# The last four rows of a weight quarter, loaded by partitions: 112 at once, then four times four

## The chip, the cores and the metric

The kernel runs on one core of one Trainium2 chip. The metric is the device time of one execution in microseconds (us).

## The reference

It is one step of grouped-query attention with a cache: 32 query heads, 8 key and value heads, a cache of 2048 positions, 8 batches with 4 tokens each, in bf16.

```python
B, Sq, D = 8, 4, 512            # x
Hq, Hkv, Sk, Dh = 32, 8, 2048, 128
q = (x @ wq).reshape(B, Sq, Hq, Dh).transpose(0, 2, 1, 3)
k = repeat(k_cache, Hq // Hkv, axis=1)
v = repeat(v_cache, Hq // Hkv, axis=1)
scores = einsum("bhqd,bhkd->bhqk", q, k) * Dh ** -0.5
p = softmax(scores)
o = einsum("bhqk,bhkd->bhqd", p, v)
out = o.transpose(0, 2, 1, 3).reshape(B, Sq, Hq * Dh) @ wo
```

## The kernel before, in words

The work is cut into 16 units, each one batch with four of the eight key/value heads (`units`). For each unit the kernel loads a K tile and a V tile of 2 MiB each (`load_k`, `load_v`), 128 partitions by 16 KB. VectorE turns the keys (`turn_keys`), TensorE makes the scores, ScalarE the exponentials, and the probabilities go back into the order of the keys (`probs_to_keys`) as copies that write 32 partitions each of one buffer. TensorE multiplies them with V (`values`); `divide` and `finish` scale and transpose the result. The loop over `n` runs 18 times: at step n it makes the scores of unit n and the values of unit n - 2.

All loads are issued by SyncE (SP), in the order of the program. `load_ready` issues the K and V tiles as their buffers come free (three of each). The last V tile is loaded in two parts, three quarters and one quarter. At step 15, behind all K and V loads, come the loads of wo, by the list `pieces`.

wo has 4096 rows of 512 elements (1024 bytes). It is taken in four quarters of 1024 rows; within a quarter, partition q holds the eight rows 8q to 8q + 7, which lie side by side in memory. `load_wo(p, r0, n)` loads the rows r0 to r0 + n - 1 of each partition's eight in quarter p:

```python
pieces = [(0, 0, 8), (1, 0, 8), (2, 0, 8), (3, 0, 4), (3, 4, 2), (3, 6, 2)]
```

The first three are 1 MiB each. The fourth, (3, 0, 4), is half of the last quarter: 128 partitions with 4096 adjoining bytes each, 512 KB. The last two are 256 KB each.

After the loop `project(p, r0, n)` multiplies the attention result with the rows of one piece, two matmuls for each r, and adds everything up in one accumulator, `out_ps`. The pieces come in the order of the list, and steps of the last unit's finishing (`finish`, `to_tokens`, `to_wo_rows`) stand between the first ones. One copy takes `out_ps` to `out_sb`, and two stores of 16 KB, one from ScalarE's queue and one from SP's, end the program. The order on each engine is the one written out (`manual_schedule`); waits between engines are put in where one instruction needs the data or the buffer of another.

Of the kernel before, what the change touches and what calls it, by code (L numbers as in the profile page):

```python
# [14 lines left out]
def kernel(  # L15
# [9 lines left out]
    nc = tc.nc  # L25
# [16 lines left out]
    NP = Hq // HP  # L42
    DH = D // 2
    NU = (Hkv // G) * B
    KB, VB, PB, LAG = 3, 3, 2, 2
    scale = float(Dh) ** -0.5
    AX = mybir.AxisListType.X
    ADD = mybir.AluOpType.add
# [52 lines left out]
    def load_wo(p, r0, n):  # L101
        rows = wo[p * HP * 128 : (p + 1) * HP * 128, :].rearrange("(q r) j -> q r j", r=WR)
        w0 = p * WR + r0
        nc.sync.dma_start(wo_sb[:, w0 : w0 + n, :], rows[:, r0 : r0 + n, :])

    load_k(0)
    nc.sync.dma_start(wq_sb[:, :, :], wq.rearrange("(p r) n -> p r n", r=R))
# [94 lines left out]
    wo_sb = wpool.tile([128, NP * WR, D], BF16, tag="w", name="wo_sb")  # L202
# [174 lines left out]
    for n in range(NU + LAG):  # L377
# [37 lines left out]
        if n == NU - 1:  # L415
            assert not loads, loads
            for piece in pieces:
                load_wo(*piece)
# [46 lines left out]
```

## Time and profile before

| what | value |
|---|---|
| median of three runs | 190.73 us (185.65 to 190.85) |
| the profiled execution | 185.65 us, span 183.9 us |
| TensorE (PE) busy | 124.5 us, 68% of the span |
| VectorE (DVE) busy | 119.3 us, 65% |
| ScalarE (ACT) busy | 83.3 us, 45% |
| GpSimd (POOL) busy | 57.2 us, 31% |
| read from memory | 75.53 MB, 411 GB/s over the span |
| share of DMA in the chain that ended last | 51% |
| mean granted TensorE clock | 0.907 |

Busy time is what an engine spent on instructions, and may lie beside that of another. The chain that ended last is followed back from the last instruction, at each step to what released it. The span is the time from the first instruction to the last; the execution's own time has 1.75 us more. DMA work is done by 16 DMA engines; a transfer has landed when the last of the engines that carry it is done.

### The profile page before, as it was taken

To read this page: it belongs to the slowest core of one execution; us is meant where nothing else is said; L and a number is where in the kernel's file an instruction comes from. 1 tells how busy PE (TensorE), PEld (TensorE's weight loads), DVE (VectorE), ACT (ScalarE), POOL (GpSimd) and SP (SyncE) were. 2 spreads that over 40 slices of the span, in tenths; PEclk is the share of its full clock that TensorE was granted. 3 is DMA by queue.
4 is the path that set the end of the run, shared out by engine and by line. 5 is a ranking of instruction groups with operands and counts; after the bars stand their busy time and mean duration, and the time that the engine had idled before them with its cause. 6 is when DMAs were issued, how large, how long until landed. Compare 5 with 4: busy or idle time off the path is not lost.

```text
span 183.9 us, 2569 instructions
## 1 busy us (share of the span) xinstructions
PE 124.5 (68%) x964; PEld 82.1 (45%) x964; DVE 119.3 (65%) x147; ACT 83.3 (45%) x154; POOL 57.2 (31%) x122
## 2 busy tenths in 40 slices
PE   0000465437959796887978858399867977499992
PEld 0000141202626574755736626247453746269770
DVE  0180234968597989989889777567857685936210
ACT  2000130272825674946847646346572638084020
POOL 8920000152405151632534515142332415056000
PEclk9999999655887999999999999958996699879999
DMA  6999999999999999999999999999999999999980
GB/s 185 471 435 389 442 417 446 417 442 428 424 442 417 446 413 437 421 435 431 428 431 428 438 413 438 438 428 435 417 442 417 442 421 435 438 411 429 421 366 19
DMA packets 5915, 75.71 MB, mean 412 GB/s; under 512 B 688, under 2 KB 784, under 8 KB 1296
## 3 DMA queue, kind: packets, MB, share of 16 engines
q1 hardware_dynamic: 5856, 75.55, 96.8%
q8 instruction: 7, 0.11, 0.2%
q14 instruction: 4, 0.03, 0.0%
q10 hardware_dynamic: 48, 0.02, 0.0%
HBM read 75.53 MB, written 0.03 MB: 411 GB/s over the span
## 4 chain that ended last, share of the span: by engine, by line
DMA 51%; DVE 30%; PE 14%; ACT 2%; issue 1%; SPq 0%; ACTq 0%; DVEq 0%
DMA k_sb<-in_k_cache_dram 24%; DVE kt L137 21%; DMA v_sb<-in_v_cache_dram 9%; DMA x_sb<-in_x_dram 9%; PE s_ps L215 9%; DMA wo_sb<-in_wo_dram 8%; DVE top L233 5%; PE o_ps L300 3%; DVE swapped L225 1%; DVE q_g L174 1%; PE psq L157 1%; DVE q_bd L193 1%; ACT q_g L172 1%; PE pse L181 1%; DVE less L239 1%
## 5 line engine op out<-in xcount | busy, mean ns | idle before, releaser
L137 DVE STREAM_TRANSPOSE kt<-k_sb 128x2048 f32<-128x2048 f32 x32 | 72.0, 2288 | 17.5 <-DMA k_sb<-in_k_cache_dram 17.4
L215 PE MATMUL s_ps<-kt,q_bd 128*64 128x512 bf16 x256 | 44.5, 479 | 33.1 <-DVE kt L137 33.1
L300 PE MATMUL o_ps<-v_sb,probs 128*128 128x256 bf16 x512 | 61.3, 281 | 0.0
L271 POOL COPY probs<-p_t 32x512 bf16<-32x512 bf16 x63 | 38.6, 612 | 59.4 <-DVE r_sb L289 57.1
L300 PEld LDWEIGHTS <-probs 128*128 128x128 bf16 x512 | 50.5, 101 | 12.1 <-issue 5.2
L271 ACT COPY probs<-p_t 32x512 bf16<-32x512 bf16 x62 | 38.1, 615 | 19.7 <-DVE r_sb L289 18.5
L215 PEld LDWEIGHTS <-q_bd 128*64 128x64 bf16 x256 | 17.3, 126 | 49.7 <-issue 25.2
L233 DVE TENSOR_REDUCE top<-s_ps 128x1 f32<-128x1024 f32 x16 | 19.6, 1224 | 16.7 <-PE s_ps L215 16.7
L251 ACT ACTIVATE s_sb<-s_ps,less 128x1024 bf16<-128x1024 f32 x16 | 22.4, 1400 | 9.8 <-DVE less L239 9.6
L225 POOL COPY l_swapped<-l_sb 64x1 f32<-64x1 f32 x32 | 5.8, 180 | 50.3 <-ACT s_sb L251 49.6
L324 ACT CAST oT<-o_t 128x64 bf16<-128x64 f32 x16 | 3.4, 212 | 33.3 <-PE o_t L323 33.3
L147 PE MATMUL xtp<-ident,x_sb 32*128 32x32 bf16 x4 | 0.3, 194 | 18.7 <-DMA x_sb<-in_x_dram 18.7
L316 ACT ACTIVATE o_sc<-o_ps,r_sb 64x128 f32<-64x128 f32 x28 | 10.1, 362 | 5.9 <-PE o_ps L300 5.7
L172 ACT ACTIVATE q_g<-psq 32x512 bf16<-32x512 f32 x4 | 2.4, 588 | 21.6 <-DVE q_g L174 21.6
L261 DVE STREAM_TRANSPOSE p_t<-s_sb 128x512 f32<-128x512 f32 x16 | 10.7, 672 | 1.6 <-ACT s_sb L251 1.6
L147 PEld LDWEIGHTS <-x_sb 32*128 32x128 bf16 x4 | 0.2, 114 | 18.7 <-DMA x_sb<-in_x_dram 18.7
L323 PEld LDWEIGHTS o_t<-both,o_sc 128*128 128x128 f32 x32 | 5.4, 211 | 7.1 <-issue 6.1
L323 PE MATMUL o_t<-both,o_sc 128*128 128x64 f32 x32 | 7.5, 320 | 0.2 <-DVE o_sc L318 0.2
L130 POOL MEMSET probs<- 128x4096 bf16 x2 | 7.0, 3511 | 0.0
L174 DVE TENSOR_SCALAR q_g<-psq 32x512 bf16<-32x512 f32 x4 | 2.7, 681 | 4.4 <-ACT q_g L172 2.3
L181 PE MATMUL pse<-ident,q_g 128*128 128x128 bf16 x32 | 3.3, 263 | 3.3 <-ACT q_g L172 2.9
L225 DVE COPY swapped<-top 64x1 f32<-64x1 f32 x32 | 4.7, 148 | 0.8
(32 smaller groups left out, 48.5 us busy)
## 6 DMA issues: line engine op xcount, KB each, us to landing
k_sb<-in_k_cache_dram SPq DMA_DIRECT2D x16, 2048.0 KB, 20.3
v_sb<-in_v_cache_dram SPq DMA_DIRECT2D x15, 2048.0 KB, 19.8
wq_sb<-in_wq_dram SPq DMA_DIRECT2D x1, 4096.0 KB, 17.3
wo_sb<-in_wo_dram SPq DMA_DIRECT2D x3, 1024.0 KB, 18.6
v_sb<-in_v_cache_dram SPq DMA_DIRECT2D x1, 1536.0 KB, 13.8
v_sb<-in_v_cache_dram SPq DMA_DIRECT2D x1, 512.0 KB, 14.6
wo_sb<-in_wo_dram SPq DMA_DIRECT2D x1, 512.0 KB, 21.3
wo_sb<-in_wo_dram SPq DMA_DIRECT2D x2, 256.0 KB, 16.9
```

The source lines that it names most:

```text
L130: nc.gpsimd.memset(pr[:, :, :, :, :, :], 0.0)
L137: nc.vector.transpose(kts[(u, t)][:, :, :, :, :].rearrange("k c h s e -> k (c h s e)").bitcast(FP32), ks[u][:, t * CT : (t + 1) * CT, :].r ...
L181: nc.tensor.matmul(pse[:, h, :, :, :].rearrange("d g b s -> d (g b s)"), lhsT=q_g[:, h, k, e, :, :].rearrange("t g w -> t (g w)"), rhs=ide ...
L215: nc.tensor.matmul(s_pss[u][h * NQ : (h + 1) * NQ, t, :, :], lhsT=q_bd[:, hq, k, e, b, :, :].rearrange("k g q -> k (g q)"), rhs=kts[(u, t) ...
L225: engine.tensor_copy(out=out[h * NQ : (h + 1) * NQ, :], in_=in_[(1 - h) * NQ : (2 - h) * NQ, :])
L233: nc.vector.reduce_max(out=top[:, :], in_=s_pss[u][:, :, :, :].rearrange("q t c s -> q (t c s)"), axis=AX,)
L251: nc.scalar.activation(out=s_sbs[u][:, :, :, :].rearrange("q a s j -> q a j s"), in_=s_pss[u][:, :, :, :].rearrange("q t (a j) s -> q (t a ...
L261: nc.vector.transpose(p_t[:, :, :, :, :].rearrange("s x g q j -> s (x g q j)").bitcast(FP32), s_sbs[u][:, :, :, :].rearrange("q a s j -> q ...
L271: by[h * G + g](out=probs[u % PB][g * S : (g + 1) * S, h, :, :, g, :], in_=p_t[quad * S : (quad + 1) * S, :, g % 2, :, :].rearrange("s x q ...
L300: nc.tensor.matmul(o_pss[u][:, :, :].rearrange("n j d -> n (j d)"), lhsT=probs[u % PB][:, h, t * CT // 4 + a, :, :, :].rearrange("s j g q ...
L316: nc.scalar.mul(out=to, in_=of, mul=by)
L323: nc.tensor.matmul(o_t[:, :], lhsT=o_scs[u][:, :], rhs=both[:, :], start=True, stop=True)
```

## The change

The load of piece (3, 0, 4) is issued as five transfers instead of one: partitions 0 to 111 in the first, then 112 to 115, 116 to 119, 120 to 123 and 124 to 127. All other pieces are loaded as before, and the same bytes go to the same places.

```diff
     KB, VB, PB, LAG = 3, 3, 2, 2
+    XE, FEW = 4, (NP - 1, 0)
...
     def load_wo(p, r0, n):
         rows = wo[p * HP * 128 : (p + 1) * HP * 128, :].rearrange("(q r) j -> q r j", r=WR)
         w0 = p * WR + r0
-        nc.sync.dma_start(wo_sb[:, w0 : w0 + n, :], rows[:, r0 : r0 + n, :])
+        to, of = wo_sb[:, w0 : w0 + n, :], rows[:, r0 : r0 + n, :]
+        if (p, r0) != FEW:
+            nc.sync.dma_start(to, of)
+            return
+        cuts = [0] + list(range(128 - 4 * XE, 129, XE))
+        for q0, q1 in zip(cuts, cuts[1:]):
+            nc.sync.dma_start(to[q0:q1], of[q0:q1])
```

With `XE` = 4 the list `cuts` is 0, 112, 116, 120, 124, 128; `NP` is 4, so `FEW` is (3, 0).

## The prediction

> **What bounds the kernel now.** I began with the chain that ended last, because the change touches only the last loads. From 111 us on it is DMA but for 12 us of keys, scores and values between 136 and 148, and its end reads (start us, length us, what):
>
> ```profile
> 148.01 17.37 DMA v_sb<-in_v_cache_dram
> 165.38 0.02 issue
> 165.40 14.73 DMA wo_sb<-in_wo_dram
> 180.13 0.04 issue
> 180.17 0.41 PE out_ps L368 x4
> 180.58 0.02 issue
> 180.60 0.36 ACT out_sb L432
> ```
>
> The last piece of wo is issued 0.02 us after a V tile has landed and lands itself at 180.13; four matmuls, one copy and the store follow. Whatever moves that landing later moves the end by as much. Between the two landings, v_cache's last tile (2 MiB) and wo (4 MiB) come in: 6.29 MB in 14.75 us, 426 GB/s, which is 26.7 GB/s for each of 16 DMA engines. One 4096-byte row (one partition's share of the piece that is cut) so costs its engine 0.154 us.
>
> Next I read the busy time by stretches over the last microseconds (the second-to-last column is the mean share of the 16 DMA engines):
>
> ```profile
> 176.00:178.00 2.00, 1.93 (x30) 1.43 (x28) 0.77 (x2) 0.65 (x2) 0.00 (x0) 1.00 0.99 402
> 178.00:178.50 0.50, 0.50 (x14) 0.50 (x11) 0.00 (x0) 0.00 (x0) 0.00 (x0) 1.00 0.85 332
> 178.50:179.00 0.50, 0.36 (x9) 0.17 (x5) 0.00 (x0) 0.00 (x0) 0.00 (x0) 1.00 0.64 246
> 179.00:179.50 0.50, 0.50 (x8) 0.31 (x5) 0.00 (x0) 0.00 (x0) 0.00 (x0) 1.00 0.47 180
> 179.50:180.00 0.50, 0.40 (x5) 0.20 (x4) 0.00 (x0) 0.00 (x0) 0.00 (x0) 1.00 0.07 25
> ```
>
> The engines don't stop together. The share falls over nearly two microseconds: a few have no more work by 178.5, a third by 179, about half by 179.3, and the rest run to about 179.7. So an early engine has room for some ten rows of 0.154 us, and a late one has none. The view doesn't say which engine is which.
>
> Then TensorE's timeline, to see whether it could use earlier data:
>
> ```profile
> 174.71 0.61 PE L368 MATMUL out_ps<-wo_sb,oP 128*32 128x256 bf16 x8
> 177.07 2.86 PE L368 MATMUL out_ps<-wo_sb,oP 128*32 128x256 bf16 x36
> 180.17 0.40 PE L368 MATMUL out_ps<-wo_sb,oP 128*32 128x256 bf16 x4 [0.23 <-DMA wo_sb<-in_wo_dram]
> ```
>
> Eight projections take 0.61 us, 0.076 each. The 36 from 177.07 on need 36 x 0.076 = 2.75 us and took 2.86, so TensorE hardly waited before the last four, and there only 0.23 us. No earlier landing can bring more than 0.23 us.
>
> Last, the waits of SP's queue (total us, times, longest):
>
> ```profile
> SPq L104 <- DMA v_sb<-in_v_cache_dram: 7.1, 2, 4.6
> ```
>
> SP issues the first four wo pieces from 156.13 at 0.47 us each, then waits: the fifth goes out at 160.49, the sixth at 165.40. The sixth leaves right after the landing of the transfer eight places before it (the V tile issued at 148.01), and the transfer eight before the fifth is the V tile issued at 136.47. I read this as: an issue waits for the transfer eight before it.
>
> **The change part by part.**
> *Four more issues on SP.* One issue takes 0.33 to 0.43 us (SP's timeline), so at most 4 x 0.43 = 1.7 us of a queue that otherwise waits from 165.73 to the store at 180.99. The eight-places rule shifts them. The transfer of 112 goes out where its piece does now. The four small ones come behind the landings of the V tiles at 160.49 and 165.38 and of the two parts of the last V tile; by bytes (2 MiB in 4.92 us) those are at about 169.1 and 170.3. The pieces (3, 4, 2) and (3, 6, 2) then wait for the first two wo pieces, at 172.8 and 175.2 (2.46 us per MiB). On the latest engine the second one's turn comes at 179.5; on the earliest, nearly 2 us before. The store of 16 KB, from a nearly empty queue, takes 1.4 us from issue to landing, so 175.2 + 1.4 = 176.6 is still before either. Cost: nothing, hidden by the queued third wo piece (2.46 us). Without that cover an early engine would pause, for at most 1.4 us, which it has.
>
> *The rows of each engine.* The piece has 128 rows, eight per engine, 1.23 us. Now 112 rows give seven each, so every engine is relieved of one row: -0.154 us. The last 16 rows come in fours. Four rows occupy four engines at most, and nothing in the trace before shows how a transfer of four is spread. Lower bound: each transfer goes to four other engines, and all have eight rows again (0); or the four engines are early ones, and the late ones keep the relief (-0.154). Upper bound, with four engines working in parallel: the same four each time, 7 + 4 = 11 rows, three more than before, +0.46 us if the latest engine is one of them. [...]
>
> I take +0.3. Half the engines run beyond 179.3, so four picked without regard to that are all early with a chance near 1/16; the latest of them is then some 0.15 us before the latest of all, and 0.46 - 0.15 = 0.31.
>
> *What waits on it.* The eight matmuls of the cut piece need five landings instead of one. They start about 178.9 now (177.07 plus 24 x 0.076); 0.3 us later they and the eight after them (1.22 us in all) end at about 180.4, and the last landing at 180.13 + 0.3 decides as before. The added waits themselves are bounded by the chain's issue gaps, 0.02 to 0.05 us each, and pass while TensorE waits for data anyway: 0. Copy and store move along unchanged.
>
> *Sum.* 0 + 0.3 + 0 on a span of 183.9 us: 184.2. The profiled execution took 185.65 us, 1.75 around its span, so 185.95. The three runs shown are 190.85, 190.73 and 185.65: the profiled one is the lowest, 5.08 below the median, with no change between them. The median is what the next kernel is held against, so I carry the +0.3 over to it: 191.0.
>
> **The rivals.**
> *Early engines* (gain). The four engines with 11 rows are early ones, and the rest finish a row sooner: -0.15, 185.5 on the profiled execution, 190.6 on the median. For it: half the engines have 0.4 us to spare or more. Against it: all four must be such.
>
> [...]
>
> *The small transfers follow one another* (slower). If their writes into one buffer are taken for overlapping, each waits for the landing of the one before. The first goes out once the 112 rows have landed (178.7), each takes the store's 1.4 us (also 16 KB), the fourth goes out at 178.7 + 3 x 1.4 = 182.9, and the two pieces behind it land about two issues and 1.4 us later, at 185.0: +4.9, 190.55 or 195.6, slower by 2.6%. It decides from the first such wait on, as the queue is empty by then. Against it:
>
> ```profile
> 151.10 2.54 ACT L271 COPY probs<-p_t 32x512 bf16<-32x512 bf16 x4 [1.09 <-DVE r_sb L289]
> 151.22 2.58 POOL L271 COPY probs<-p_t 32x512 bf16<-32x512 bf16 x4 [4.32 <-DVE r_sb L289]
> ```
>
> Two engines write different partitions of one buffer side by side, with no wait for each other.
>
> *The spread of the runs.* Without any change runs lie 5.2 us apart. The new median may land near the low one: 185.65 + 0.3 = 185.95, 2.5% under the old median, though nothing was gained; or be judged against the low one and count as slower.
>
> **How the numbers follow.** Forecast (+0.3) 0.42; early engines 0.14; one place for four rows 0.14; one after another 0.08; the spread 0.22, of which 0.14 show as faster and 0.08 as slower. Within 2% (3.8 us, about what a measurement of this kernel can tell from no change) are the first three: 0.70. Faster by more: 0.14, from the spread alone, since the trace allows no gain over 0.23 us. Slower: 0.08 + 0.08 = 0.16. The range goes from the low run less the relief, 185.65 - 0.15 = 185.5, to the rate limit's 192.1; left out are the serial case and part of the spread. The likeliest case by itself is 190.6 to 191.2 (-0.15 to +0.46).
>
> **What would show it.** In the changed profile: SP issues ten transfers at L104's successor, the last two about 172.8 and 175.2; the DMA share thins out earlier on most engines (below 0.47 in 179.0 to 179.5) with a tail of a few engines to about 180.0; the last wo landing is at 180.4. A landing at 180.0 means early engines; after 181, a rate limit; small transfers issued after 178, the serial case. A change of the rate before 170 us would mean that my account misses something.

## The result, and the profile after

The changed kernel is slower: its time is 1.0119 times that of the kernel before (95% interval 1.0107 to 1.0132), +2.2 us on 185.6. Both kernels have longer runs too (in the first profile of the changed kernel, which is of such a run, the loads run for a long stretch at some 376 GB/s), so the ratio compares the undisturbed runs, and the lines below come from a second profile of the changed kernel, taken with the first experiments. There it took 1.0103 times the time before (1.0085 to 1.0120), 187.5 us against 185.7.

The chain that ended last, of that second profile (start us, length us, what):

```profile
156.59 18.61 DMA wo_sb<-in_wo_dram
175.20 0.02 issue
175.21 6.55 DMA wo_sb<-in_wo_dram
181.77 0.04 issue
181.81 0.41 PE out_ps L375 x4
182.22 0.02 issue
182.24 0.36 ACT out_sb L439
```

The last landing of wo moved from 180.13 to 181.77 us, +1.64, and everything behind it moved along: that is nearly all of the loss. The last issue now follows a landing of wo at 175.20, as the eight-places rule said.

Busy time by stretches, first the kernel before and then the changed one (the two last columns are the DMA engines' mean busy share and GB/s):

```profile
174.00:176.00 2.00, 1.75 (x26) 1.26 (x24) 0.30 (x2) 0.51 (x2) 0.00 (x0) 1.00 0.97 410
176.00:177.00 1.00, 0.94 (x16) 0.68 (x12) 0.34 (x1) 0.34 (x2) 0.00 (x0) 1.00 0.96 399
177.00:178.00 1.00, 0.99 (x17) 0.75 (x17) 0.42 (x1) 0.30 (x1) 0.00 (x0) 1.00 1.01 406
178.00:179.00 1.00, 0.86 (x17) 0.67 (x15) 0.00 (x0) 0.00 (x0) 0.00 (x0) 1.00 0.75 289
179.00:180.00 1.00, 0.90 (x12) 0.51 (x9) 0.00 (x0) 0.00 (x0) 0.00 (x0) 1.00 0.27 102
```

```profile
174.00:176.00 2.00, 1.76 (x22) 1.17 (x20) 0.70 (x2) 0.42 (x2) 0.00 (x0) 1.00 0.97 408
176.00:177.00 1.00, 1.00 (x20) 0.79 (x16) 0.28 (x1) 0.50 (x1) 0.00 (x0) 1.00 1.11 324
177.00:178.00 1.00, 0.94 (x18) 0.69 (x14) 0.17 (x2) 0.34 (x2) 0.00 (x0) 1.00 0.94 201
178.00:179.00 1.00, 0.69 (x12) 0.49 (x10) 0.40 (x1) 0.11 (x1) 0.00 (x0) 1.00 1.02 227
179.00:180.00 1.00, 0.85 (x16) 0.56 (x12) 0.00 (x0) 0.00 (x0) 0.00 (x0) 1.00 0.81 178
180.00:181.00 1.00, 0.12 (x3) 0.15 (x5) 0.00 (x0) 0.00 (x0) 0.00 (x0) 1.00 0.58 211
```

Up to 176 us the two agree. Then, in the changed kernel, the DMA engines stay as busy as before but move little more than half: 201 GB/s at a share of 0.94 and 227 at 1.02, where the kernel before moves 406 at 1.01. The engines together don't have more rows to carry; a row takes nearly twice as long. The traces hold the time of every single row too. In the kernel before all 128 rows of the piece take 0.159 us or so; in the changed kernel 90 of the 128 take over 0.2 us, and the median is 0.27 us. The timeline of TensorE in the changed kernel shows who pays:

```profile
177.87 0.61 PE L375 MATMUL out_ps<-wo_sb,oP 128*32 128x256 bf16 x8
178.80 1.05 PE L375 MATMUL out_ps<-wo_sb,oP 128*32 128x256 bf16 x16 [0.31 <-DMA wo_sb<-in_wo_dram]
180.88 1.32 PE L375 MATMUL out_ps<-wo_sb,oP 128*32 128x256 bf16 x16 [1.04 <-DMA wo_sb<-in_wo_dram]
```

The projections, which ran almost without a break before, now wait for the third piece (0.31 us) and for the cut one (1.04). The third piece isn't cut, and it too is late: the slow stretch begins before it has landed.

### The profile page after: what moved, and what is told of

Read it like the earlier page. It is cut to its first block, busy times and chain, and to the rows that moved or that the text cites. A ratio compares the mean times of both kernels' runs of the same rounds, so it can differ in the third digit from the quotient of the medians.

```text
span 193.5 us, 2575 instructions
## 1 busy us (share of the span) xinstructions
PE 128.7 (67%) x964; PEld 83.9 (43%) x964; DVE 119.7 (62%) x147; ACT 83.3 (43%) x154; POOL 57.2 (30%) x122
## 4 chain that ended last, share of the span: by engine, by line
DMA 59%; DVE 23%; PE 13%; ACT 2%; SPq 1%; issue 1%; ACTq 0%; DVEq 0%
DMA k_sb<-in_k_cache_dram 37%; DVE kt L144 16%; DMA wo_sb<-in_wo_dram 13%; DMA x_sb<-in_x_dram 9%; PE s_ps L222 8%; DVE top L240 3%; PE o_ps L307 2%; DVE q_g L181 1%; PE psq L164 1%; DVE q_bd L200 1%; ACT q_g L179 1%; PE pse L188 1%; DVE swapped L232 1%; ACT s_sb L258 1%; PE o_t L330 1%
## 5 line engine op out<-in xcount | busy, mean ns | idle before, releaser
L222 PE MATMUL s_ps<-kt,q_bd 128*64 128x512 bf16 x256 | 47.3, 503 | 37.6 <-DVE kt L144 37.6
L307 PE MATMUL o_ps<-v_sb,probs 128*128 128x256 bf16 x512 | 62.3, 283 | 0.0
L222 PEld LDWEIGHTS <-q_bd 128*64 128x64 bf16 x256 | 18.1, 130 | 55.1 <-issue 28.2
L330 PEld LDWEIGHTS o_t<-both,o_sc 128*128 128x128 f32 x32 | 6.0, 235 | 7.8 <-issue 6.8
L330 PE MATMUL o_t<-both,o_sc 128*128 128x64 f32 x32 | 8.3, 348 | 0.2 <-DVE o_sc L325 0.2
L375 PE MATMUL out_ps<-wo_sb,oP 128*32 128x256 bf16 x64 | 4.6, 274 | 1.4 <-DMA wo_sb<-in_wo_dram 1.3
```

The costliest lines, as they stand in the source:

```text
L222: nc.tensor.matmul(s_pss[u][h * NQ : (h + 1) * NQ, t, :, :], lhsT=q_bd[:, hq, k, e, b, :, :].rearrange("k g q -> k (g q)"), rhs=kts[(u, t) ...
L307: nc.tensor.matmul(o_pss[u][:, :, :].rearrange("n j d -> n (j d)"), lhsT=probs[u % PB][:, h, t * CT // 4 + a, :, :, :].rearrange("s j g q ...
L330: nc.tensor.matmul(o_t[:, :], lhsT=o_scs[u][:, :], rhs=both[:, :], start=True, stop=True)
```

## The experiments

Three theories stood against each other. *Shared places*: a DMA engine is slowed where another one writes to neighbouring partitions at the time, a guess to explain the 253 GB/s at a share of 1.02 from 184 to 186 us in the first profile of the changed kernel. *Rows*: only the number of rows on each engine counts, 0.154 us each. *Late issues*: the last two pieces are issued too late. Times are given as the ratio to the kernel before on the same chip and, times 185.7 us, in microseconds. All edits are in the branch of `load_wo` for the piece (3, 0, 4), written with `to` and `of` as in the change, but for two that cut another piece and one `memset`, which stand with their runs.

**The changed kernel once more**

> The changed kernel once more, for a second look at its tail. Theory of shared places (engines that write neighbouring partitions share the rate of one engine, and the transfer of 112 partitions, seven rows per engine, no longer gives each engine a place of its own): about 2.2 us over the kernel before; from the start of the 112 transfer the engines stay busy (share near 1) while they move only some 250 GB/s instead of 425. Theory of rows (four engines carry eleven rows instead of eight, at an unchanged 0.154 us): the rate per busy engine stays at 26 GB/s, and the end moves by at most 0.46 us. Theory of late issues (the last two pieces wait for the transfer eight places before them): the DMA share falls below 1 before those two pieces start.

Measured: 1.0103 (1.0085 to 1.0120), +1.9 us, and the lines above: the share near 1 and 201 to 227 GB/s. That is what shared places expected. By rows alone the rate per busy engine would have stayed, and a row would have kept its time.

**One transfer for the last 16 partitions**

```diff
+        nc.sync.dma_start(to[:112], of[:112])
+        nc.sync.dma_start(to[112:], of[112:])
```

> 112 partitions in one transfer, the last 16 in one transfer. If it spreads one row on each of 16 engines, every engine has eight rows as before. [...] Rows: 0, within 0.1. Late issues: the last two pieces then wait for V tiles that landed long before, so 0.

Measured: 1.0102 (1.0074 to 1.0131), +1.9 us. Without any transfer of four the loss is as large as with them. Rows and late issues expected 0.

**Two halves of 64 neighbours**

```diff
+        nc.sync.dma_start(to[:64], of[:64])
+        nc.sync.dma_start(to[64:], of[64:])
```

> The piece in two transfers of 64 neighbouring partitions, four rows on each of 16 engines in both. [...] Rows: 0. Late issues: 0.

Measured: 1.0114 (1.0089 to 1.0139), +2.1 us. No odd count and no small transfer, and still the whole loss; more than the +1.2 that half of the 426 GB/s for this piece alone would make (2.46 us for its 512 KB instead of 1.23). Its stretches:

```profile
177.00:178.00 1.00, 0.94 (x16) 0.58 (x14) 0.42 (x1) 0.57 (x1) 0.00 (x0) 1.00 0.95 219
178.00:179.00 1.00, 1.00 (x20) 0.92 (x20) 0.42 (x1) 0.37 (x1) 0.00 (x0) 1.00 1.07 260
179.00:180.00 1.00, 0.85 (x16) 0.52 (x12) 0.00 (x0) 0.00 (x0) 0.00 (x0) 1.00 0.82 201
```

**The whole piece, and four transfers of four in addition**

```diff
+        nc.sync.dma_start(to, of)
+        spare = q_g[:, :, :, :, :, :].rearrange("q a b c d e -> q (a b c d e)")
+        for q0 in range(112, 128, 4):
+            nc.sync.dma_start(
+                spare[q0 : q0 + 4, :], of[q0 : q0 + 4].rearrange("q r j -> q (r j)")
+            )
```

> The piece whole (128 partitions, as before), and behind it the four transfers of four partitions once more, into a buffer that is no longer used: 64 KB in addition, no transfer of 112. Rows: four rows more on four engines, up to 4 x 0.154 = +0.61 us. [...] Late issues: the last two pieces go out as late as in the changed kernel, so if that is the cause the full +2.2 comes back without the 112 transfer.

Measured: 1.0038 (1.0021 to 1.0054), +0.7 us. In size this is about what four more rows on four engines do (0.61), but rows alone would have kept the rate, and it is lower in one stretch:

```profile
178.00:179.00 1.00, 0.76 (x14) 0.57 (x11) 0.00 (x0) 0.00 (x0) 0.00 (x0) 1.00 0.80 209
```

The kernel before moves 289 GB/s there at a share of 0.75. How the 0.7 divides between more rows and slower ones, the run doesn't tell. The late issue of the last two pieces, which comes with the small transfers, can't cost more than that: that theory falls.

**Even and odd partitions**

```diff
+        nc.sync.dma_start(to[0::2], of[0::2])
+        nc.sync.dma_start(to[1::2], of[1::2])
```

> The piece in two transfers of 64 partitions again, but the even ones in the first and the odd ones in the second, each from its own rows. [...] Theory of small transfers (every transfer of fewer than 128 partitions runs slowly, whichever they are): +2.1, as with the halves.

Measured: 1.0001 (0.9990 to 1.0011), 0.0 us. The same two transfers of 64 partitions cost nothing when they don't take neighbours:

```profile
177.00:178.00 1.00, 0.44 (x10) 0.25 (x6) 0.26 (x1) 0.00 (x0) 0.00 (x0) 1.00 1.00 395
178.00:179.00 1.00, 0.96 (x16) 0.68 (x15) 0.00 (x0) 0.00 (x0) 0.00 (x0) 1.00 0.71 277
179.00:180.00 1.00, 0.79 (x12) 0.59 (x13) 0.00 (x0) 0.00 (x0) 0.00 (x0) 1.00 0.35 133
```

395 GB/s where the halves have 219: the stretch runs as in the kernel before. Row by row it is the same: in the halves 112 of the piece's 128 rows take over 0.2 us, here none does.

**Source and destination crossed**

```diff
+        nc.sync.dma_start(to[:64], of[0::2])      # dst_halves
+        nc.sync.dma_start(to[64:], of[1::2])
...
+        nc.sync.dma_start(to[0::2], of[:64])      # src_halves
+        nc.sync.dma_start(to[1::2], of[64:])
```

> Two transfers into the partitions 0 to 63 and 64 to 127, as in the halves, but read from the even and the odd groups of rows, so that wo's rows lie in the wrong partitions. If the sharing is where the rows are written: +2.1 us as with the halves. [...]

> The other way round: written to the even and the odd partitions, read from the first and the second half of the rows, so that wo's rows lie in the wrong partitions. [...] Sharing where it is read: +2.1.

Measured: halves on the destination's side 1.0125 (1.0105 to 1.0145), +2.3 us; halves on the source's side 1.0004 (0.9992 to 1.0015), +0.1. So it is the partitions written to that decide, and the order of the addresses read doesn't matter.

**The transfer of 112 alone**

```diff
+        nc.sync.dma_start(to[:112], of[:112])
...
+        if n == 8:
+            nc.gpsimd.memset(wo_sb[96:, (NP - 1) * WR : (NP - 1) * WR + 4, :], 0.0)
```

> Only the transfer of 112 partitions; the other 16 partitions of the piece are set to zero by GpSimd long before, so that an eighth of the piece is left out. [...] Theory of rows: each engine is relieved of one row, -0.154 us, and only the four-row transfers could bring a loss.

Measured: 1.0086 (1.0058 to 1.0114), +1.6 us, with an eighth of the piece left out. A stretch of it, and TensorE's last projections:

```profile
177.00:178.00 1.00, 0.12 (x4) 0.00 (x0) 0.03 (x1) 0.00 (x0) 0.00 (x0) 1.00 0.98 238
178.68 3.40 PE L372 MATMUL out_ps<-wo_sb,oP 128*32 128x256 bf16 x32 [1.56 <-DMA wo_sb<-in_wo_dram]
```

The transfer of 112 makes most of the loss by itself, with 64 KB less to load: 238 GB/s at a share of 0.98, and 83 of its 112 rows take over 0.2 us. Not all of the 1.6 is the loads'. TensorE waited 1.56 us for the third piece, its granted clock went to 0.50, and its last 32 projections took 3.40 us where 2.43 (32 x 0.076) was usual. The last landing by itself came at 181.43 us, 1.30 later than in the kernel before.

**Eleven rows, but no neighbours**

```diff
+        for q0, q1, step in ((0, 128, 2), (1, 96, 2)):
+            nc.sync.dma_start(to[q0:q1:step], of[q0:q1:step])
+        for q0 in range(97, 104, 2):
+            nc.sync.dma_start(to[q0::8], of[q0::8])
```

> The same rows per engine as in the changed kernel by count (seven on each, four rows more on four engines), but with partitions that don't lie side by side: 64 even ones (four rows each), 48 odd ones below 96 (three each), and the last 16 odd ones in four transfers of four, eight partitions apart. Theory: the sharing of places made most of the changed kernel's +2.0 us, and the rows the rest, so +0.3 to +0.8. If uneven counts of rows or transfers of four are themselves what costs: +2.0 as in the changed kernel.

Measured: 1.0054 (1.0036 to 1.0072), +1.0 us, half of the changed kernel's loss at the same number of rows per engine, and a little over what was expected. Some sharing is left, it seems (from 177 to 178 us it moves 287 GB/s at a share of 0.87, 330 per full share, where the kernel before has 400, and 24 of the 128 rows take over 0.2 us); how much of the 1.0 it is, the run doesn't tell.

**The four-row transfers, four partitions apart**

```diff
+        nc.sync.dma_start(to, of)
...
+        for i in range(4):
+            nc.sync.dma_start(
+                spare[112 + i :: 4, :], of[112 + i :: 4].rearrange("q r j -> q (r j)")
+            )
```

> As the whole piece with four transfers of four added behind it (+0.7 us), but each of them with partitions four apart (112, 116, 120, 124 and so on), into a buffer that is no longer used. If the four-row transfers cost by their four rows on four engines alone: 4 x 0.154 = 0.61 at most, +0.4 to +0.7. If half of their +0.7 came from four rows in one place, less: +0.3 to +0.5.

Measured: 1.0043 (1.0025 to 1.0061), +0.8 us, no less than with neighbours (+0.7), and the stretch from 178 to 179 us is as slow as with them (207 GB/s at a share of 0.81). Whether their four rows lie side by side makes no difference that these runs show.

**The halves in a piece of another size**

```diff
-        if (p, r0) != (NP - 1, 0):      # halves
+        if (p, r0) != (NP - 1, 6):      # halves_last: 256 KB
...
+        if (p, r0) != (0, 0):           # halves_first: 1 MiB
```

> The last piece of wo (256 KB, two rows of 1024 bytes in each partition) in two transfers of 64 neighbouring partitions; all others whole. Shared places with a cost by bytes: half of the halves' +2.1, about +1.0 us (+0.6 to +1.2). A cost per transfer, whatever its size: +2.1.

> The first piece of wo (1 MiB, eight rows in each partition) in two transfers of 64 neighbouring partitions, about 5 us before the end of the loads; all others whole. Cost by bytes and kept to the end, as the loads behind it only follow in the queue: twice the halves' +2.1, +2.5 to +4.2 us. A cost per transfer: +2.1. If what is lost is given back by the pieces behind it: under +1.

Measured: 256 KB 1.0115 (1.0023 to 1.0207), an interval of +0.4 to +3.8 us, which tells nothing apart; 1 MiB 1.0238 (1.0213 to 1.0262), +4.4 us, twice the +2.1 of 512 KB, and not given back by the 3 MiB behind it. Its stretches:

```profile
168.00:170.00 2.00, 2.00 (x20) 1.79 (x19) 0.70 (x2) 1.09 (x2) 0.97 (x2) 1.00 1.20 240
170.00:171.00 1.00, 1.00 (x12) 0.92 (x10) 0.45 (x2) 0.21 (x1) 0.00 (x0) 1.00 0.80 160
171.00:172.00 1.00, 1.00 (x11) 0.90 (x10) 0.25 (x1) 0.00 (x0) 0.00 (x0) 1.00 1.08 258
172.00:174.00 2.00, 2.00 (x21) 1.80 (x19) 0.00 (x0) 0.00 (x0) 0.00 (x0) 1.00 1.08 205
174.00:176.00 2.00, 0.33 (x4) 0.19 (x2) 0.70 (x2) 0.21 (x1) 0.00 (x0) 1.00 0.97 213
176.00:177.00 1.00, 0.00 (x0) 0.00 (x0) 0.00 (x0) 0.00 (x0) 0.00 (x0) 1.00 0.92 229
177.00:178.00 1.00, 0.25 (x6) 0.24 (x8) 0.00 (x0) 0.00 (x0) 0.00 (x0) 1.00 0.98 393
```

From 168 to 177 us it moves 1963 KB (each rate times its length), 218 GB/s instead of 426, with the engines busy: 9 x (1 - 218/426) = 4.4 us lost, the whole difference. At half the rate the piece alone would take 4.9 us; the slow stretch lasts nine. My reading is that the engines, whose ends lie nearly 2 us apart, enter and leave the two halves at different times and meet each other longer than if they came together; that is argued, not shown.

**Four transfers of 32**

```diff
+        for q0 in range(0, 128, 32):            # quarters
+            nc.sync.dma_start(to[q0 : q0 + 32], of[q0 : q0 + 32])
...
+        for i in range(4):                      # four_apart
+            nc.sync.dma_start(to[i::4], of[i::4])
```

> The piece in four transfers of 32 neighbouring partitions, two rows on each engine in each. [...] Places in the order of the partitions (32 neighbours are a quarter of the places): a quarter of the rate, 524,288 bytes at 107 GB/s are 4.9 us instead of 1.23, +3.7 us or more.

> The piece in four transfers of 32 partitions, each with every fourth partition, two rows on each engine in each. Shared places: all places are reached, so 0 to +0.3 us, as with the even and odd ones. A cost of the number of transfers, or of the last two pieces' late issue (they then wait for the first two pieces of wo, as in the changed kernel): as the quarters, +2 or so.

Measured: 32 neighbours 1.0155 (1.0141 to 1.0170), +2.9 us; every fourth partition 1.0013 (0.9995 to 1.0030), +0.2 us. The second settles that neither the number of transfers nor their being of 32 partitions costs much, since only the partitions differ (it moves 404 GB/s at a share of 1.02 from 182 to 183 us of its profile). The first came out between the halves' +2.1 and the +3.7 of a quarter of the rate. The stretches of the kernel with neighbours (PEclk, the granted clock of TensorE, is the third column from the end):

```profile
177.00:178.00 1.00, 0.26 (x6) 0.08 (x1) 0.17 (x1) 0.00 (x0) 0.00 (x0) 1.00 0.89 184
178.00:179.00 1.00, 0.00 (x0) 0.00 (x0) 0.00 (x0) 0.00 (x0) 0.00 (x0) 0.85 1.05 260
179.00:180.00 1.00, 0.56 (x6) 0.47 (x7) 0.00 (x0) 0.00 (x0) 0.00 (x0) 0.50 0.87 211
```

The rate is about that of the halves, 184 to 260 GB/s, and not the 107 of a quarter. Why 32 neighbours come at the rate of 64, no run here shows. A part of the 0.8 us that they cost beyond the halves is TensorE's:

```profile
179.44 1.89 PE L373 MATMUL out_ps<-wo_sb,oP 128*32 128x256 bf16 x16 [2.19 <-DMA wo_sb<-in_wo_dram]
```

It waited 2.19 us for the third piece, which isn't cut; its clock went to 0.50, and these 16 projections took 1.89 us where 1.22 was usual, and so did the last 16.

## Why the prediction was wrong

- *What bounds the kernel, and where TensorE stands*: right. The last landing decided, and the end moved with it.
- *Issues on SP*: right. Ten issues, the last two at 172.73 and 175.2 as worked out, and no idle share before their turn; the whole piece with four transfers of four behind it issues its last two pieces just as late, and lost only 0.7 us.
- *The rows of each engine*: the step that failed. It took the 112 rows as a gain of 0.154 us on every engine, with an unchanged 0.154 us per row. The 112 transfer alone costs +1.6 us, and the last landing alone is 1.30 us later with it: its rows come at little more than half the rate (0.26 us in the median, where 0.159 was usual). I had bounded the unknown by the four-row transfers alone, and let the row of the 128-partition transfers stand for one of 112.
- *The four small transfers*: of about the size taken, +0.7 us when added to the whole piece, near the 0.61 of four rows on four engines (0.46 after the relief that the forecast set against them), and the smaller of the two terms. But it is not the unchanged price per row that was summed. That the four transfers go to the same four engines, as the +0.46 has it, no run shows outright; what they show in its place is landings in four parts. In the changed kernel the first of these transfers lands in four parts, at 177.76, 178.99, 179.71 and 180.00 us, the second at 178.05, 179.24, 179.95 and 180.21, and so on, as rows one behind another on the same four engines would. That fits the upper bound's eleven rows on four engines, but such a row took 0.21 to 0.34 us, not 0.154. That the sizes agree is in part luck.
- *The rivals*: the rate limit, with a chance of 0.14, stood for 192.1, +1.4, with a landing after 181 us as its sign, and the sign came (181.77). It was right in kind, a rate and not a count. But it put the limit into the transfers of four, and no run shows that term: the loss is as large with no transfer of four at all (+1.9), and four rows taken four partitions apart cost as much as neighbours (+0.8 and +0.7). What the runs show in its place is the wide transfer's low rate, 238 GB/s at a share of 0.98 with the 112 alone. One after another and early engines fall: the first by the issues of the small transfers, the last at 170.3 us, long before 178, the second by the sign of the result.
- *The number*: 191.0 stood for +0.3 us over the kernel before, and +2.2 was measured: within 2%, as I had thought likeliest, but clear of no change. That the sign came out is no credit to the sum, whose term for the 112 rows had the other sign.

What the cause rests on: the same counts of rows and transfers cost +2.1 us or nothing, by the partitions written to (halves against even and odd, crossed, 32 neighbours against every fourth), and where it costs nothing no row of the piece takes over 0.2 us. That the 112 transfer is slow for the same reason is the reading that fits, since it is slow by itself and shows the same low rate at full share; which engine writes which partition in it was not seen. No version here beat the kernel before: its piece in one transfer of 128 is as fast as any.

## What to carry to other kernels

A busy DMA share didn't mean full speed here, so read it beside the GB/s of the same stretch: half the rate at a share near 1 (201 GB/s at 0.94, where the kernel before moved 406 at 1.01) meant slower rows (0.27 us in the median for 0.159), not more of them. Before a load is split by partitions, ask which partitions each part is written to: here parts of 64 or 32 neighbours ran at about half the rate (219 to 260 and 184 to 260 GB/s), parts of every second or fourth of the 128 partitions at the full one (395 and 404). And the price per row read from 128-partition transfers didn't hold for the transfer of 112 (0.26 us in the median for 0.159), even though it has fewer rows for each engine.

## What the hardware showed that I had not expected

Leaving out an eighth of a piece made the kernel 1.6 us slower. The slow stretch reaches into transfers that aren't cut: the third wo piece, whole, landed late in the changed kernel (TensorE waited 0.31 us for it, and 2.19 in the kernel with 32 neighbours), and a piece of 1 MiB cut in halves slowed the loads for nine microseconds (218 GB/s where 426 was usual). And in that wait of 2.19 us TensorE's granted clock fell to 0.50, which made its last projections half again as long (1.89 us for 1.22); with the transfer of 112 alone it fell likewise in a wait of 1.56 us, while after 1.04 us in the changed kernel it stayed at 1.00. Whether the wait is what lowers it, no run here was made to tell.
